# FFN matmuls of 128 x 128 as two column halves of 64, implied waits left out, first loads in parts

## The chip, the cores and the metric

One core of one Trainium2 chip runs the whole program. The metric is the device time of that program in microseconds (us). A profiled execution gives, beside its time, a trace of every engine: TensorE (PE for its matmuls, PEld for the loads of their stationary operand), VectorE (DVE), ScalarE (ACT), GpSimd (POOL) and SyncE (SP), which issues most of the DMAs.

## The reference

Attention with a threshold for 8 sequences of 8 heads (576 tokens, 64 wide), and an FFN with an ELU over all 4608 tokens.

```python
scores = scale * np.matmul(q, k.transpose(0, 1, 3, 2))
thresh = np.max(scores, axis=-1, keepdims=True) - tau
scores = np.where(scores >= thresh, scores, -1000000000.0)
scores = scores - np.max(scores, axis=-1, keepdims=True)
attn = np.exp(scores)
attn = attn / (np.sum(attn, axis=-1, keepdims=True) + 1e-09)
x = np.matmul(attn, v)            # then (B, S, H*D): 4608 x 512
h = x @ w_in                      # 512 x 2048
g = np.where(h > 0.0, h, np.exp(np.minimum(h, 0.0)) - 1.0)
return g @ w_out                  # 2048 x 512
```

## The kernel before

All is fp32. A sequence has four pairs of heads, so there are 32 pairs. Of the 576 tokens, 512 are four blocks of 128 and 64 are the tail; the tails of all eight sequences together make a ninth FFN group (`xtail`).

**Attention.** A step takes 128 queries of a pair. PE writes the scores to PSUM (`scores`, L494, in the first sequence; `wide_scores`, L769, and the tails, L816, later), in tiles of 64 rows by 64 columns: the two heads stand on different rows of the array, and the 128 queries are two halves of 64 columns, so up to four tiles lie side by side. DVE takes the negated maximum (L518, L776), POOL makes the threshold `th` from it (L522, L782), ACT the exponential (L528, L786), DVE masks and sums (L538, L790), POOL or ACT divides. The result is transposed by DVE and a trip through DRAM (`turn_squares`, `fetch`), or by PE (`turn_parts`), and multiplied with the values (`values`, L708 and L713; `tails_and_values`, L821 and L829). L713 and L829 write 64 columns for each head, so two matmuls of 128 rows by 64 columns lie side by side. L708, ahead of L713, covers both heads with a block-diagonal `vd` of 128 by 128.

**FFN.** The first pairs' FFN (`ffn1`, `ffn1_block`, `ffn2_plain`) is plain. From about 256 us on each group of 512 tokens goes through `first_product` (L1447: seven products of 2 x 2 blocks in place of eight, after Strassen and Winograd) and `second_round` (L1587, likewise); for the last groups `deep_product` (L1961, one level deeper, products of 128 columns) and `plain_product` (L2023). Each product is matmuls of 128 x 128 weights by 256 or 128 columns into a PSUM bank, then copies and sums on ACT, DVE and POOL. In the profile one fp32 matmul is two MATMUL records and two LDWEIGHTS.

**Order of the work.** Every engine runs its instructions in the order in which the program lists them. For the first sequence and the pairs up to the ninth the order is the string `EARLY`, one entry a job: `ld.tail.1.0` is the load of the k tails, `ld.k.0.0:act` a load issued by ACT, `idle17@f0` 17 transposes of the identity that only keep PE running, `first.q.0.0@f0` a transpose into bank f0, `sc.n` the scores of step n, `th.n.h` a threshold (its first engine, POOL, unless the entry names one). After that, a schedule by planned times (`at`, `until`, `on_pe`) lays FFN quarters between the attention steps: for each pair, tails and values, the scores of two blocks, FFN, the scores of the other two, FFN.

**Waits.** An instruction that reads or writes the wide PSUM tile is registered by `on_banks` (L720), which makes it wait for the other engines' accesses to the same bank. An instruction with more waits than it can carry gets an EVENT_SEMAPHORE instruction ahead of it on its queue.

**First loads.** `load_one` (L1108) gives source and place of a load; `load_job` (L1123) makes a job of it, on SP or ACT. Before, q of a block and the tails of q or k come in one load for all eight heads.

Of the kernel before, what the change touches and what calls it, by code (L numbers as in the profile page):

```python
# [60 lines left out]
ld.tail.1.0 ld.k.0.0:act ld.k.0.1 ld.tau.0.0:act idle17@f0 ld.q.0.0 ld.k.1.1 ld.k.1.0 lw.0 lw.1 first.t.k.0@f0  # L61
# [115 lines left out]
def kernel(  # L177
# [12 lines left out]
    P = 128  # L190
# [268 lines left out]
    WBUFS = 3  # L459
    e_both, e_next = att.tile([P, 2, 2, HALF], FP32, name="e", bufs=1), [0]  # L460
# [59 lines left out]
    def bound_of(pr, i, h):  # L520
        st = open_steps[pr, i]
        nc.gpsimd.tensor_scalar(st["th"][:, h : h + 1], st["mx"][:, h : h + 1], -1.0, ntau, ALU.mult, ALU.add)  # L522

    def exp_of(pr, i, h):
        st = open_steps[pr, i]
        e = e_slot()
        o = st[h][:, :, :HALF]
        on_banks(nc.scalar.activation(e, o, AF.Exp, bias=st["mx"][:, h : h + 1]), o)  # L528
        st[h] = st[h], e
# [169 lines left out]
    def values(pr, part, pv=None, block=None):  # L699
        b, j = divmod(pr, NPAIR)  # L700
        vm, vd = (raws[pr][x] for x in ("vm", "vd"))
        wT = wTs.pop((pr, part) if block is None else (pr, "block", block))
        if b not in xts:
            xts[b] = xpool.tile([P, KJ, MAIN], FP32, name="xt")
        n = wT.shape[1] * T
        if pv is None:
            pv = granted[0]
        watch(nc.tensor.matmul(pv[:, :n], vd, wT[:, :, NC], start=True, stop=False, skip_group_check=True), pv[:, :n])  # L708
        for c in range(NC):
            for h in range(2):  # L710
                g0, g1 = (2 * h, 2 * h + 10) if part else (0, wT.shape[1])
                o = pv[h * D : (h + 1) * D, g0 * T : g1 * T]
                watch(nc.tensor.matmul(o, vm[:, h, c], wT[:, g0:g1, h * (NC + 1) + c], start=False, stop=(c == NC - 1),  # L713
                                       skip_group_check=True), o)
        return lambda e="act": values_out(pr, part, pv, block, e)

    seen = const.tile([P, 1], FP32, name="seen")
    accesses, banked, doing, after = {}, {}, [None], [()]

    def on_banks(made, ap):  # L720
# [11 lines left out]
        needed += [i for y in after[0] for i in banked.get(y, {}).values() if str(i.engine) != engine and i not in needed]  # L732
        if doing[0]:
            banked.setdefault(doing[0], {})[engine] = ins
# [6 lines left out]
        tc.add_to_no_dep_group(engine, ins)  # L741

# [37 lines left out]
    def wide_bounds(pr, i):  # L780
        st, cs = open_steps[pr, i], slice(0, len(heads_of(i)))
        nc.gpsimd.tensor_scalar(st["th"][:, cs], st["mx"][:, cs], -1.0, ntau, ALU.mult, ALU.add)  # L782
# [277 lines left out]
    def early_tasks():  # L1060
# [47 lines left out]
        def load_one(what, z, h):  # L1108
# [3 lines left out]
            if what == "q":  # L1112
                return w_out_sb[:, NPAIR + z].rearrange("p (h d) -> p h d", d=D), q[0, :, z * P : (z + 1) * P].rearrange("h p d -> p h d")
            if what == "tail":
                return first_tails("qk"[z]), (q, k)[z][0, :, MAIN:].rearrange("h t d -> t h d")
# [19 lines left out]
        for c in range(NC):  # L1135
            load_job("q", c)
        load_job("tail", 0), load_job("tail", 1), load_job("tau")
        job("tau", "dve", lambda e: read_tau(), "ld.tau.0.0")
        for pr in range(NPAIR):
            for name, part, cs in (("k", 0, range(NC)), ("q", 0, (0,)), ("q", 1, (1, 2, 3))):  # L1140
# [3 lines left out]
                    *[("ld", "k", pr, h) for h in range(2) if name == "k"], *[("ld", "q", c, 0) for c in cs if name == "q"],  # L1144
                    bank=("prep", name, pr, part))
                job(("prep", name, pr, part), "act|dve", lambda e, loc=loc: loc["out"](e), x, "tau" if name == "q" else None)
            for z, name in enumerate("qk"):
                loc = {}
                job(("first", "t", name, pr), "pe", lambda e, pr=pr, name=name, loc=loc: loc.update(out=turn_first_tail(name, pr)),
                    ("ld", "tail", z, 0), bank=("copy", name, pr))  # L1150
                job(("copy", name, pr), "act|dve", lambda e, loc=loc: loc["out"](e), ("first", "t", name, pr), "tau" if name == "q" else None)
# [37 lines left out]
        for n in range(per_seq):  # L1189
# [6 lines left out]
            for h in hs:  # L1196
# [4 lines left out]
                job(("th", n, h), "pool", lambda e, pr=pr, i=i, h=h: bound_of(pr, i, h), ("max", n, h), "tau")  # L1201
# [69 lines left out]
        for z, (pr, what) in enumerate((pr, what) for pr in range(NPAIR, START) for what in ("tail", 0, 1)):  # L1271
# [23 lines left out]
            for s, (i, hs, wb) in enumerate(group_steps):  # L1295
# [6 lines left out]
                job(("bth", pr, i), "pool", lambda e, pr=pr, i=i: wide_bounds(pr, i), *[("bmax", pr, i, h) for h in hs])  # L1302
# [80 lines left out]
    with tc.manual_schedule():  # L1383
# [42 lines left out]
        def first_product(g, u):  # L1426
# [6 lines left out]
            def product(k):  # L1433
# [12 lines left out]
                for j in range(2):  # L1446
                    nc.tensor.matmul(loc["banks"][place], left[:, j], right[:, j], start=(begins and j == 0), stop=(j == 1),  # L1447
                                     skip_group_check=True)
# [108 lines left out]
        def second_round(g, r):  # L1557
            banks_ = []

            def chunk(c):  # L1560
# [5 lines left out]
                def quarter(m, k):  # L1566
# [15 lines left out]
                    for v in range(2 * k, 2 * k + 2):  # L1582
# [4 lines left out]
                        nc.tensor.matmul(place(m), lhs, rhs, start=(begins and v == 0), stop=(v == RU - 1),  # L1587
                                         skip_group_check=True)
# [352 lines left out]
        def deep_product(q):  # L1941
# [9 lines left out]
            def p(k):  # L1951
# [8 lines left out]
                for v in range(2):  # L1960
                    nc.tensor.matmul(loc["x"][place][:, :P], left[:, v], right[:, v], start=(begins and v == 0), stop=(v == 1),  # L1961
                                     skip_group_check=True)
# [49 lines left out]
        def plain_product(q):  # L2012
# [3 lines left out]
            def p(c, k):  # L2016
# [5 lines left out]
                for v in range(2 * k, 2 * k + 2):  # L2022
                    nc.tensor.matmul(loc[c][:, :HM], lefts(g, r, c, m)[:, v], rights(r, m)[:, v], start=(v == 0), stop=(v == RU - 1),  # L2023
                                     skip_group_check=True)
# [107 lines left out]
```

## Time and profile before

| | us |
|---|---|
| median of 3 runs | 1264.27 |
| lowest, highest | 1262.33, 1265.05 |
| the profiled execution | 1262.88 |
| its span, first to last instruction | 1261.1 |
| granted clock of TensorE | 1.000 |

In the profile, a line such as "L1447 PE MATMUL f<-xt,sw 128*128 128x256 f32 x512" names the line of the kernel, the engine, the operation, the tiles written and read, the rows and columns of the array in use, the result's partitions and columns, and the number of records. The chain of waits is followed back from the last instruction: at each step to what released it, or to the instruction before it on its engine. Matmuls are pipelined and their ends are modelled; their starts are not, so intervals between starts are the safer measure.

### The profile page before, as it was taken

To read this page: it belongs to the slowest core of one execution; us is meant where nothing else is said; L and a number is where in the kernel's file an instruction comes from. 1 tells how busy PE (TensorE), PEld (TensorE's weight loads), DVE (VectorE), ACT (ScalarE), POOL (GpSimd) and SP (SyncE) were. 2 spreads that over 40 slices of the span, in tenths; PEclk is the share of its full clock that TensorE was granted. 3 is DMA by queue.
4 is the path that set the end of the run, shared out by engine and by line. 5 is a ranking of instruction groups with operands and counts; after the bars stand their busy time and mean duration, and the time that the engine had idled before them with its cause. 6 is when DMAs were issued, how large, how long until landed. Compare 5 with 4: busy or idle time off the path is not lost.

```text
span 1261.1 us, 24668 instructions
## 1 busy us (share of the span) xinstructions
PE 1245.4 (99%) x8187; PEld 970.9 (77%) x8187; DVE 1068.6 (85%) x2322; ACT 584.7 (46%) x1276; POOL 788.6 (63%) x1147
## 2 busy tenths in 40 slices
PE   8999999999999999999999999999999999999998
PEld 5776576477777777777788777777777778899998
DVE  6998989898889979898989888988989885777876
ACT  7987755453444435252625353444535260434130
POOL 5775545586576747674767657674757473675554
PEclk9999999999999999999999999999999999999999
DMA  9568898898989898999889898989889876434433
GB/s 225 147 180 240 226 260 244 240 306 213 254 212 262 233 244 223 260 245 237 241 225 268 218 268 202 269 221 251 215 255 248 237 215 219 166 133 150 143 107 112
DMA packets 332880, 277.84 MB, mean 220 GB/s; under 512 B 201296, under 2 KB 288336, under 8 KB 332752
## 3 DMA queue, kind: packets, MB, share of 16 engines
q1 hardware_dynamic: 331760, 275.73, 78.8%
q8 instruction: 65, 1.06, 0.3%
q10 hardware_dynamic: 992, 0.53, 0.1%
q14 instruction: 63, 0.52, 0.1%
HBM read 178.85 MB, written 97.32 MB: 219 GB/s over the span
## 4 chain that ended last, share of the span: by engine, by line
PE 82%; DVE 3%; issue 1%; ACT 0%; DMA 0%; SPq 0%; POOL 0%; DVEq 0%; ACTq 0%
PE f L1447 30%; PE f L1587 23%; PE sc L829 9%; PE sc L769 8%; PE f L1961 4%; PE f L2023 3%; PE sc L821 1%; PE f L888 1%; PE sc L816 1%; DVE mx L776 1%; PE f L956 1%; DVE x L641 1%; DVE e L790 0%; DVE w_one L790 0%; DMA there<-x 0%
## 5 line engine op out<-in xcount | busy, mean ns | idle before, releaser
L776 DVE TENSOR_REDUCE mx<-sc 128x1 f32<-128x576 f32 x252 | 180.2, 746 | 37.8 <-PE sc L769 32.3
L782 POOL TENSOR_SCALAR th<-mx,ntau 128x2 f32<-128x2 f32 (+1 forms) x140 | 46.0, 329 | 187.1 <-DVE mx L776 186.9
L786 ACT ACTIVATE w_one<-sc,mx 128x576 f32<-128x576 f32 x140 | 100.8, 741 | 132.7 <-DVE mx L776 113.3
L790 DVE SCALAR_TENSOR_TENSOR w_one<-sc,th,w_one 128x576 f32<-128x576 f32 x140 | 110.0, 813 | 20.4 <-ACT w_one L786 20.2
L769 PE MATMUL sc<-kT,qT 64*64 64x256 f32 (+5 forms) x1792 | 124.2, 410 | 2.4 <-DVE su L546 0.5
L1447 PE MATMUL f<-xt,sw 128*128 128x256 f32 x512 | 123.8, 384 | 0.6 <-ACT xt L432 0.5
L786 ACT ACTIVATE e<-sc,mx 128x576 f32<-128x576 f32 x112 | 82.8, 743 | 86.6 <-DVE mx L776 85.0
L1447 PE MATMUL f<-x,w_in_sb 128*128 128x256 f32 x512 | 122.8, 382 | 0.0
L1447 PE MATMUL f<-xt,w_in_sb 128*128 128x256 f32 x512 | 121.2, 379 | 0.5 <-DVE xt L1056 0.5
L769 PEld LDWEIGHTS sc<-kT,qT 64*64 64x64 f32 x1792 | 80.7, 132 | 48.3 <-issue 18.2
L502 POOL TENSOR_SCALAR w_one<-w_one,rs 128x576 f32<-128x576 f32 x115 | 89.4, 788 | 38.7 <-DVE rs L552 38.7
L641 DVE STREAM_TRANSPOSE x<-w_one 128x512 f32<-128x512 f32 (+1 forms) x140 | 99.9, 744 | 14.2 <-POOL w_one L502 9.5
L1447 PEld LDWEIGHTS f<-xt,sw 128*128 128x128 f32 x512 | 94.1, 190 | 21.1 <-issue 5.8
L1447 PEld LDWEIGHTS f<-x,w_in_sb 128*128 128x128 f32 x512 | 96.2, 190 | 16.2 <-ACT g L1508 3.6
L1447 PEld LDWEIGHTS f<-xt,w_in_sb 128*128 128x128 f32 x512 | 97.2, 190 | 14.0 <-ACT e L786 0.8
L790 DVE SCALAR_TENSOR_TENSOR e<-sc,th,e 128x576 f32<-128x576 f32 x112 | 87.7, 808 | 8.3 <-ACT e L786 7.9
L1587 PE MATMUL f<-w_out_sb,g 128*128 128x256 f32 x384 | 92.0, 382 | 0.0
L1587 PE MATMUL f<-w_out_sb,s 128*128 128x256 f32 x384 | 91.9, 382 | 0.0
L1587 PE MATMUL f<-t,s 128*128 128x256 f32 x384 | 90.7, 379 | 0.0
L1587 PEld LDWEIGHTS f<-w_out_sb,g 128*128 128x128 f32 x384 | 72.0, 190 | 13.1 <-issue 3.8
L1587 PEld LDWEIGHTS f<-w_out_sb,s 128*128 128x128 f32 x384 | 71.9, 190 | 12.7 <-issue 3.2
L502 POOL TENSOR_SCALAR e<-e,rs 128x576 f32<-128x576 f32 x92 | 67.8, 742 | 20.8 <-DVE rs L552 18.3
(344 smaller groups left out, 2894.1 us busy)
## 6 DMA issues: line engine op xcount, KB each, us to landing
there<-x SPq DMA_DIRECT2D x452, 144.0 KB, 3.8
wTb<-there SPq DMA_DIRECT2D x58, 576.0 KB, 6.4
wTa<-there SPq DMA_DIRECT2D x55, 576.0 KB, 4.7
sw<-win_sums SPq DMA_DIRECT2D x62, 384.0 KB, 4.3
t<-wout_sums SPq DMA_DIRECT2D x45, 512.0 KB, 5.3
there<-x SPq DMA_DIRECT2D x112, 80.0 KB, 1.9
wTb<-there SPq DMA_DIRECT2D x56, 160.0 KB, 3.6
wst<-in_moe_w_in_dram SPq DMA_DIRECT2D x16, 512.0 KB, 4.8
```

The costliest lines, as they stand in the source:

```text
L502: nc.gpsimd.tensor_scalar(wv, wv, st["rs"][:, h : h + 1], 1.0, ALU.mult, ALU.mult)
L641: nc.vector.transpose(x[:, :, c0 : c0 + nc_], src.rearrange("p (c g n) -> p g c n", c=nc_, n=T))
L769: on_banks(nc.tensor.matmul(oy, qT[r, i * P + y * D : i * P + (y + 1) * D], kT[r, k0 : k0 + n], start=True, stop=True, skip_group_check=Tr ...
L776: on_banks(nc.vector.tensor_reduce(st["mx"][:, h : h + 1], st["sc", h], axis=AX.XY if i == NC else AX.X, op=ALU.max, negate=True), st["sc" ...
L782: nc.gpsimd.tensor_scalar(st["th"][:, cs], st["mx"][:, cs], -1.0, ntau, ALU.mult, ALU.add)
L786: on_banks(nc.scalar.activation(st["e", h], st["sc", h], AF.Exp, bias=st["mx"][:, h : h + 1]), st["sc", h])
L790: on_banks(nc.vector.scalar_tensor_tensor(st["e", h], st["sc", h], st["th"][:, h : h + 1], st["e", h], ALU.is_ge, ALU.mult, accum_out=st[" ...
L829: on_banks(nc.tensor.matmul(o, vm[:, h, c], parts[part][:, g0:g1, h * (NC + 1) + c], start=False, stop=(c == NC - 1), skip_group_check=Tru ...
L1447: nc.tensor.matmul(loc["banks"][place], left[:, j], right[:, j], start=(begins and j == 0), stop=(j == 1), skip_group_check=True)
L1587: nc.tensor.matmul(place(m), lhs, rhs, start=(begins and v == 0), stop=(v == RU - 1), skip_group_check=True)
L1961: nc.tensor.matmul(loc["x"][place][:, :P], left[:, v], right[:, v], start=(begins and v == 0), stop=(v == 1), skip_group_check=True)
L2023: nc.tensor.matmul(loc[c][:, :HM], lefts(g, r, c, m)[:, v], rights(r, m)[:, v], start=(v == 0), stop=(v == RU - 1), skip_group_check=True)
```

## The change

It has four parts.

1. FFN matmuls go through the new `by_columns`, which makes two matmuls of 128 rows by 64 columns of one of 128 by 128. This holds for `first_product` (L1447), `second_round` (L1587), `deep_product` (L1961), `plain_product` (L2023), and for the first matmul of `values` (L708). The moving operand is read by both halves.
2. `on_banks` drops a wait that another one implies, by the new `followed`; and in `exp_of` the dependence on the exponential that used the same slot before is dropped, since a mask lies between.
3. The loads of q's first block and of the k tails are split: heads 0 and 1, then heads 2 to 7. The first line of `EARLY` is rearranged for it.
4. Thresholds may be made by ACT (`bound_of`, `wide_bounds`); no entry of `EARLY` asks for it.

```diff
 EARLY = """
-ld.tail.1.0 ld.k.0.0:act ld.k.0.1 ld.tau.0.0:act idle17@f0 ld.q.0.0 ld.k.1.1 ld.k.1.0 lw.0 lw.1 first.t.k.0@f0
+ld.tail.1.1 ld.k.0.0:act ld.k.0.1 ld.q.0.1:act ld.tau.0.0 ld.tail.1.2:act idle17@f0 ld.q.0.2 ld.k.1.1 ld.k.1.0 lw.0 lw.1 first.t.k.0@f0
...
     def exp_of(pr, i, h):
         st = open_steps[pr, i]
         e = e_slot()
         o = st[h][:, :, :HALF]
-        on_banks(nc.scalar.activation(e, o, AF.Exp, bias=st["mx"][:, h : h + 1]), o)
+        made = nc.scalar.activation(e, o, AF.Exp, bias=st["mx"][:, h : h + 1])
+        if slot_exps[e_next[0]]:
+            tc.declare_no_dep(made.ins, slot_exps[e_next[0]].name, reason="its mask lies between")
+        slot_exps[e_next[0]] = made.ins
+        on_banks(made, o)
...
-        watch(nc.tensor.matmul(pv[:, :n], vd, wT[:, :, NC], start=True, stop=False, skip_group_check=True), pv[:, :n])
+        by_columns(pv[:, :n], vd, wT[:, :, NC], watch, start=True, stop=False)
...
+    serials, known = {}, {}
+
+    def followed(ins, engine, needed):
+        have = known.setdefault(engine, {})
+        kept_ = []
+        for x in needed:
+            e, n, _ = serials[x.name]
+            if n > have.get(e, -1) and not any(serials[y.name][2].get(e, -1) >= n for y in needed if y is not x and serials[y.name][0] != e):
+                kept_.append(x)
+        for x in kept_:
+            e, n, seen = serials[x.name]
+            for z, m in {**seen, e: n}.items():
+                have[z] = max(have.get(z, -1), m)
+        serials[ins.name] = engine, len(serials), dict(have)
+        return kept_
...
+        needed = followed(ins, engine, needed)
...
+    def by_columns(o, left, right, note=None, **how):
+        n = o.shape[0]
+        for y in range(0, n, D):
+            oy = o[y : y + D] if n > D else o
+            made = nc.tensor.matmul(oy, left[:, y : y + D] if n > D else left, right, skip_group_check=True, **how)
+            if note:
+                note(made, oy)
...
             if what == "q":
-                return w_out_sb[:, NPAIR + z].rearrange("p (h d) -> p h d", d=D), q[0, :, z * P : (z + 1) * P].rearrange("h p d -> p h d")
+                hs = (slice(0, H), slice(0, 2), slice(2, H))[h]
+                return w_out_sb[:, NPAIR + z].rearrange("p (h d) -> p h d", d=D)[:, hs], q[0, hs, z * P : (z + 1) * P].rearrange("h p d -> p h d")
...
                 for j in range(2):
-                    nc.tensor.matmul(loc["banks"][place], left[:, j], right[:, j], start=(begins and j == 0), stop=(j == 1),
-                                     skip_group_check=True)
+                    by_columns(loc["banks"][place], left[:, j], right[:, j], start=(begins and j == 0), stop=(j == 1))
```

The replacements at L1587, L1961 and L2023 are of the same form.

41 lines of the change are left out of this document (24 added, 17 removed).

## The prediction

> **What bounds the kernel now.** I read the busy line and the chain of waits on the page first, then the busy time by stages, then the chain in order of time, and last single stretches of the timeline of TensorE.
>
> ```profile
> PE 1245.4 (99%) x8187; PEld 970.9 (77%) x8187; DVE 1068.6 (85%) x2322; ACT 584.7 (46%) x1276; POOL 788.6 (63%) x1147
> PE 82%; DVE 3%; issue 1%; ACT 0%; DMA 0%; SPq 0%; POOL 0%; DVEq 0%; ACTq 0%
> 300.00:700.00 400.00, 400.00 (x2651) 314.23 (x2652) 351.32 (x774) 175.08 (x384) 261.29 (x395) 1.00 0.90 241
> 700.00:1038.00 338.00, 338.00 (x2206) 266.45 (x2200) 294.31 (x647) 147.91 (x323) 216.61 (x329) 1.00 0.86 236
> ```
>
> The columns of the two stage rows are the stretch, its length, and the busy time of PE, PEld, DVE, ACT and POOL. From 300 to 1038 us PE is busy in every microsecond, DVE in 351.32 of 400 (88%). The granted clock is 1.00. The chain names PE with 82%. So from 300 us on the time is the sum of what TensorE streams and of what it loses between streams, and a change to TensorE's work counts one for one. The chain in order of time (start, length, what) gives the period:
>
> ```profile
> 219.76 1.53 DVE w_one L790 x4
> ...
> 320.21 4.03 PE sc L829 x32
> 324.24 2.09 PE sc L769 x24
> 326.33 12.30 PE f L1447 x56
> 338.63 2.09 PE sc L769 x24
> ...
> 1117.28 1.73 PE f L2023 x8
> 1119.01 1.34 PE f L1961 x12
> ```
>
> One pair of heads is values, scores, FFN, scores, FFN. An fp32 matmul leaves two records. A 256-column record takes 1.73/8 = 0.216 us in L2023, a 128-column one 1.34/12 = 0.1117 us in L1961. Each of these runs begins with a change of the array's shape, and what such a beginning costs is seen in the timeline of PE. A matmul's end is modelled, so I take the start-to-start interval: the length of a row less one matmul (0.38 us at 256 columns), over the intervals in it.
>
> ```profile
> 964.83 0.38 PE L1447 MATMUL f<-x,w_in_sb 128*128 128x256 f32 x1
> 965.14 0.45 PE L816 MATMUL sc<-kT,qT 64*64 64x288 f32 x1
> ...
> 965.96 0.38 PE L821 MATMUL sc<-wTa,vd 64*64 64x256 f32 x1
> 966.27 2.38 PE L829 MATMUL sc<-wTb,vm 128*64 128x320 f32 x16
> 968.47 1.90 PE L829 MATMUL sc<-wTa,vm 128*64 128x256 f32 x16
> 970.30 2.49 PE L769 MATMUL sc<-kT,qT 64*64 64x448 f32 x32
> ...
> 972.72 1.56 PE L1587 MATMUL f<-w_out_sb,g 128*128 128x256 f32 x6
> ...
> 974.55 1.46 PE L1587 MATMUL f<-t,g 128*128 128x256 f32 x6
> ```
>
> Three things are in these rows. First, a change of shape costs 0.09 us whichever way it goes: 964.83 to 965.14 and 965.96 to 966.27 are each 0.31 where a 256-column record has 0.216. Second, the first 128*128 run loses more behind it: (1.56 - 0.38)/5 intervals sum to 1.18 against 5 x 0.216 = 1.08, so 0.10 us is lost once, while the later row has (1.46 - 0.38)/5 = 0.216 and loses nothing. That is the first weight load, which has nothing to hide behind. Third, column halves are already in this kernel: L829 works on 128*64, two halves side by side. Its 16 records of 256 columns are 8 pairs, (1.90 - 0.38)/7 = 0.217 us for a pair, the same as one 128*128 record. Its first row, after a change of shape, has 7 intervals in 2.38 - 0.44 = 1.94; at 0.217 x 320/256 = 0.271 they would take 1.89, so only 0.05 us is lost there.
>
> **The change part by part.**
>
> (a) FFN runs in column halves. In the steady stretch a pair of halves takes what one record took (0.217 against 0.216), so 0. At the beginning of a run the exposed load falls from 0.10 to 0.05: the means of one load say the same.
>
> ```profile
> L1447 PEld LDWEIGHTS f<-xt,sw 128*128 128x128 f32 x512 | 94.1, 190 | 21.1 <-issue 5.8 <-DMA there<-x 1.2 <-ACT xt L432 0.9
> L829 PEld LDWEIGHTS sc<-wTa,vm 128*64 128x64 f32 x448 | 32.2, 137 | 19.2
> ```
>
> That is 190 against 137 ns, 0.053 less. The chain has 44 such runs of 56 between the two rows here (two every 34.0 us, 22 pairs):
>
> ```profile
> 292.38 12.31 PE f L1587 x56
> ...
> 1021.09 12.44 PE f L1447 x56
> ```
>
> 44 x 0.053 = 2.3 us. The change of shape itself stays: scores work on 64*64 and FFN on 128*64 after it, and 64*64 to 128*64 at 966.27 costs the same 0.09.
>
> (b) Eleven runs take 12.44 instead of 12.30. The extra 0.14 sits inside them, where a wait on ACT lets the queue of loads run dry:
>
> ```profile
> 957.13 2.03 PE L1447 MATMUL f<-x,w_in_sb 128*128 128x256 f32 x8
> ```
>
> 7 intervals in 2.03 - 0.38 = 1.65 against 1.51. About 0.10 of the 0.14 is again an exposed load, and half of it goes: 11 x 0.053 = 0.6 us, if ACT is no later than now (0 if it is).
>
> (c) Where values are followed directly by FFN, 128*64 meets 128*64 and the change of shape goes too. From 1037.64 + 1.03 - 0.38 = 1038.29 to 1038.61 are 0.32, so 0.10, and the load behind it, 0.10: 0.2 us once.
>
> ```profile
> 1037.64 1.03 PE L829 MATMUL sc<-wTa,vm 128*64 128x256 f32 x8
> 1038.61 1.56 PE L1587 MATMUL f<-w_out_sb,g 128*128 128x256 f32 x6
> ```
>
> (d) The 128-column products of L1961 take 0.1117 us a record. Pairs of halves of that size are in the first sequence:
>
> ```profile
> 27.15 0.49 PE L708 MATMUL sc<-wTa,vf 128*128 128x128 f32 x2
> 27.57 1.09 PE L713 MATMUL sc<-wTa,vm 128*64 128x128 f32 x16
> 1100.00:1253.00 153.00, 56.62 (x476) 56.38 (x476) 1.00 0.40 129
> ```
>
> (1.09 - 0.28 - 0.05)/7 = 0.109 us a pair, 0.0027 less, and the last row counts 476 records of L1961: 1.2 us. At the ends: 0 and 2 us.
>
> (e) The first matmul of the early values (L708, 24 records) becomes halves, so the change of shape between it and L713 and its own exposed load go: its two records take 0.42 (27.15 to 27.57) where two pairs at a beginning need 0.22 + 0.05, and L713 behind them has no beginning of its own any more (0.05): 0.20 us x 12 = 2.4 us of PE. Before 280 us the chain also runs over DVE (219.76 above), so between 0 and 2.4 lies on the path; I take 0.4, the low side, because filler transposes of the identity stand in that stretch and take up what comes free.
>
> (f) First loads in parts. The head 0/1 parts of q and of the k tails land earlier, but PE has no use for them earlier:
>
> ```profile
> 1.46 3.89 PE L555 MATMUL f<-ident 128*128 128x128 f32 x17 [1.46 <-POOL ident masks.py:199]
> 4.38 0.15 DVE L240 TENSOR_SCALAR pos<-tau_sb 128x1 f32<-128x1 f32 x1 [4.38 <-DMA tau_sb<-in_tau_dram]
> 5.27 0.18 PEld L405 LDWEIGHTS f<-ident,w_out_sb 64*128 64x128 f32 x1 [0.33 <-issue]
> 6.24 0.60 PE L555 MATMUL f<-ident 128*128 128x128 f32 x4
> 6.67 0.73 PE L555 MATMUL f<-ident,w_out_sb 128*128 128x128 f32 x2
> 6.98 0.37 ACT L426 ACTIVATE x<-f,keep 128x128 f32<-128x128 f32 x1
> 7.54 0.71 PE L494 MATMUL sc<-x 64*64 64x288 f32 x8
> ```
>
> The 17 fillers last until 5.35 by the model and hold the first real transpose at 5.27 whatever has landed; the 4 fillers hold q's at 6.67, and both fillers stay. So 0 for the loads. What is moved: ACT issues two more loads (0.5 us each, before its first copy), SP takes tau's after two others, about 1 us later, so L240 starts near 5.4 and its five operations end near 6.2, still ahead of 6.98, where ACT first needs them. SP has one load more in all, so weight loads behind it issue about 0.5 us later. Cover gone, that is at worst 0.7 us; if q was late after all, up to 0.5 us gain. I take 0.
>
> (g) Implied waits left out: an instruction with two waits has an extra one on its queue ahead of it.
>
> ```profile
> L769 PEldq EVENT_SEMAPHORE  x18: 51/51/51, 131.1 to 970.5; - x18
> L816 PEldq EVENT_SEMAPHORE  x16: 51/51/51, 143.0 to 963.1; - x16
> L790 DVEq EVENT_SEMAPHORE  x88: 21/21/21, 120.6 to 1010.6; - x88
> ```
>
> At most 34 x 0.051 = 1.7 us on PE and 88 x 0.021 = 1.8 us on DVE. On PE the one before 965.14 hides in the 0.31 of the change of shape; DVE has its 12% of idle time from 300 us on. I take 0.3, of 0 to 1.7. The choice of engine for the bounds is not used: no entry of the order names it.
>
> **Sum:** 2.3 + 0.6 + 0.2 + 1.2 + 0.4 + 0 + 0.3 = 5.0 us. The profiled execution took 1262.88 us (span 1261.1 and 1.8 around it), so 1257.9; it lies 1.4 under the median of 1264.27, from which the sum is 1259.3. I forecast 1259.
>
> **The rivals.**
>
> *TensorE's queue cannot issue that fast (slower).* Loads and matmuls double: 4 instructions a pair. At 256 columns that is 54 ns each, at 128 columns in L1961 27 ns each. The fastest stretch of the trace:
>
> ```profile
> 290.20:291.90 1.70, 1.70 (x30) 1.37 (x32) 1.34 (x5) 0.53 (x2) 1.70 (x2) 1.00 0.80 218
> ```
>
> 30 matmuls and 32 loads in 1.70 us are 27 ns an instruction, for 62 of them. Over a whole run of scores (32 matmuls, as at 970.30, and as many loads, in the 2.09 us of the chain) it is 32.7 ns. If that were the limit, a pair in L1961 would cost 4 x 32.7 = 131 ns, 19 more than now, x 476 = 9.1 us, against the 3.8 us of (a), (b), (c), (e) and (g): 1264.3 + 5.3 = 1269.6. It decides from 4 x 30 = 120 ns on, where 476 x 0.008 eats the rest. For it: no run of 27 ns longer than 62 instructions is in the trace. Against it: the scores are bound by what they stream, not by issue, so 32.7 is only the slowest that the limit can be.
>
> A rule of the Trainium skill speaks for this rival (TensorE: Matmul & The Clock Gate, Part 2): the sequencer may spend about 62 ns on each MATMUL, which binds when the array's work on one is shorter. Two halves would then cost 124 ns, 12 more than L1961 now, an estimated 5.9 us on 476, and the sum would be 1266.4. The trace speaks against it for short runs: L713's eight pairs took 109 ns each.
>
> *The gain is turned into waits (no change).* From 300 to 1038 us DVE works 88% of the time and waits for ACT already sit in eleven runs (b). If each period is held by such a wait, what PE saves there becomes idle time of PE, and only what lies behind 1038 us stays: (c) and (d), 1.4 us, 1264.3 - 1.4 = 1262.9. For it: (b). Against it: PE has no idle time in 738 us, and the saving is 0.12 us in a period of 34.
>
> *More of the early part counts.* If PE is the bound before 280 us after all, (e) gives 2.4, (g) 1.7 and (f) 0.5: 3.9 us more than in the sum, 1255.4. For it: PE stands in the chain there too. Against: so does DVE, and the fillers keep PE busy with nothing.
>
> *The halves do not overlap in FFN.* L829 has its two halves on different moving data; in FFN both stream the same. If they ran one after the other, 3136 records of 256 columns (L1447 and L1587) would cost 0.216 us more each, over 600 us. Only L829 and L713 speak on it, and both overlap; 1 in 100.
>
> **How the numbers follow.** Forecast 0.62, more of the early part 0.10, turned into waits 0.17, queue 0.10, no overlap 0.01. The forecast's own range is 1256.5 to 1261.5, from (b), (d), (e) and (g) at their ends and the 1.4 us between profile and median. The range for 8 in 10 takes in the early case below and the case without change above, and leaves out the queue: 1254.5 to 1265. About 0.2% (2.5 us) is what a measurement of this kernel can tell from no change; below 1261.7 is faster. Forecast and early case lie there, but for the upper edge of the forecast: 0.72. The case of waits is the same, with the edges: 0.17. Slower: 0.11, the queue and the case without overlap.
>
> **What would show it.** (a): in the chain, L1587 and L1447 runs of 12.25 instead of 12.30, the same 0.217 a pair within, mean load near 137 ns, and 0.31 still between scores and FFN. (b): the eleven long runs at 12.39 or below. (c): no gap at 1038. (d): L1961 at 0.109 a pair; 0.12 or more is the queue. (e): 128*128 gone from L708 and no 0.09 between it and L713. (f): the first score still at about 7.5 us. (g): fewer waits of 51 ns in L769 and L816. Wrong would be: idle time of PE between 300 and 1038 us, or an interval within FFN over 0.22 us.

## The result, and the profile after

The changed kernel takes 1259.09 us (median of 6 runs, 1258.30 to 1259.56) where the kernel before, in 6 runs beside it, takes 1263.76: a ratio of 0.9965, with a 95% interval from 0.9955 to 0.9974. (The ratios here and below, to which the intervals belong, are not the quotients of the medians; that would be 0.9963 here.) The forecast was 1259.0. The profiled execution took 1258.30 us with a span of 1256.5, which is 4.6 less than the span of before. Both profiled executions are among the shorter ones of their kernel.

The busy line and the chain's shares come from the page of the changed kernel, the last two rows from its busy time by stages.

```profile
PE 1240.8 (99%) x11999; PEld 825.9 (66%) x11999; DVE 1067.2 (85%) x2322; ACT 584.4 (47%) x1276; POOL 790.5 (63%) x1147
PE 81%; DVE 2%; DMA 1%; POOL 1%; ACT 0%; issue 0%; SPq 0%; DVEq 0%; ACTq 0%; POOLq 0%
...
300.00:700.00 400.00, 399.89 (x3970) 253.79 (x3968) 351.42 (x775) 175.27 (x385) 262.54 (x396) 1.00 0.89 242
700.00:1034.00 334.00, 334.00 (x3294) 212.52 (x3292) 291.88 (x644) 147.16 (x320) 213.81 (x324) 1.00 0.87 237
```

TensorE issues 3812 matmuls more and is still, nearly everywhere, what the time is the sum of. Weight loads take 145 us less of busy time, but they were hidden before: only the first load of a run was not. Every matmul that goes through `by_columns` stands at one line now, L772; L802 are the scores, L852 and L857 the tails, L865 the values, L563 the transposes. The chain in order of time (start, length, what) shows a period and the end of the steady part:

```profile
319.08 4.03 PE sc L865 x32
323.11 2.09 PE sc L802 x24
325.20 12.25 PE f L772 x112
337.45 2.09 PE sc L802 x24
339.54 12.35 PE f L772 x112
...
1031.70 4.03 PE sc L865 x32
1035.73 24.17 PE f L772 x224
```

Values and scores are what they were (4.03 and 2.09). An ordinary FFN run went from 12.30 to 12.25, a long one from 12.44 to 12.35. The timeline of TensorE (start, length, engine, line, what, count) shows where the 0.05 is:

```profile
963.18 0.38 PE L857 MATMUL sc<-wTa,vd 64*64 64x256 f32 x1
963.49 2.38 PE L865 MATMUL sc<-wTb,vm 128*64 128x320 f32 x16
965.69 1.90 PE L865 MATMUL sc<-wTa,vm 128*64 128x256 f32 x16
967.52 2.55 PE L802 MATMUL sc<-kT,qT 64*64 64x448 f32 x32
970.00 1.95 PE L772 MATMUL f<-w_out_sb,g 128*64 128x256 f32 x16
971.77 1.90 PE L772 MATMUL f<-t,g 128*64 128x256 f32 x16
...
1033.84 1.90 PE L865 MATMUL sc<-wTa,vm 128*64 128x256 f32 x16
1035.56 1.68 PE L772 MATMUL f<-w_out_sb,g 128*64 128x256 f32 x14
```

The FFN row at 970.00 is the first of a run: 7 intervals in 1.95 - 0.38 = 1.57, where the row behind it has 1.52. So 0.05 is lost at the beginning where it was 0.10, and within the run a pair of halves takes 1.52/7 = 0.217. Single starts say the same for all 45 runs between 290 and 1062 us: from the first product of a run to the second it is 0.320 us in the kernel before and 0.267 here (0.216 at 1035.56, see below), and 0.216 from the second to the third in both. The change of shape stays at 0.31 (963.18 to 963.49, and from 965.69 + 1.90 - 0.38 = 967.21 to 967.52). At 1035.56 there is none: 1033.84 + 1.90 - 0.38 = 1035.36, and 0.20 later FFN begins, an ordinary interval.

At the end of the program stand the products of 128 columns:

```profile
1235.87 0.64 PE L772 MATMUL f<-t,e 128*64 128x128 f32 x8
1236.30 0.64 PE L772 MATMUL f<-x,e 128*64 128x128 f32 x8
1236.74 0.64 PE L772 MATMUL f<-t,wTb 128*64 128x128 f32 x8
1237.17 0.64 PE L772 MATMUL f<-x,wTb 128*64 128x128 f32 x8
1237.61 1.93 PE L772 MATMUL f<-w_out_sb,s 128*64 128x256 f32 x16
```

Four groups of four pairs lie between 1235.87 and 1237.61: 1.74/16 = 0.109 us a pair, where one whole record took 0.1117.

To see where the time was won, I subtract, for the same row of scores or values, its start in the kernel before from its start here. All profiled kernels are in one table; their edits are in the next section. Columns are the times of those rows in the kernel before, in us, and the last one is the span.

| kernel | 7.5 (first score) | 35.6 | 131 | 270 | 286 | 407 | 422 | 1034.6 | span 1261.1 |
|---|---|---|---|---|---|---|---|---|---|
| changed | -0.43 | -0.75 | -1.06 | -1.39 | -1.09 | -1.40 | -1.48 | -2.94 | -4.6 |
| changed, again | -0.33 | -0.64 | -0.91 | -1.39 | -0.02 | -0.32 | -0.29 | -0.85 | -2.5 |
| halves alone | +0.29 | +0.30 | +0.26 | +0.19 | -0.09 | -0.47 | -0.55 | -2.32 | -3.7 |
| waits alone | +0.29 | -0.03 | -0.35 | -0.60 | +0.90 | +1.23 | +1.23 | +1.19 | +0.7 |
| loads alone | +0.44 | +0.44 | +0.46 | +0.50 | +0.06 | +0.04 | +0.04 | -0.00 | -0.4 |
| loads alone, again | +0.15 | +0.16 | +0.13 | +0.14 | -0.06 | -0.08 | -0.08 | -0.05 | -0.6 |
| changed, fillers | -0.67 | +0.16 | -0.15 | -0.63 | -1.15 | -1.50 | -1.58 | -2.98 | -4.6 |
| halves in all FFN | +0.50 | +0.16 | +1.01 | +1.69 | +1.47 | +1.15 | +2.72 | +2.89 | +1.1 |
| all but `ffn1_block` | +0.05 | -0.27 | -0.23 | +1.06 | +1.86 | +1.56 | +1.92 | +0.59 | -1.1 |
| quarters | -0.33 | -0.66 | -0.50 | +0.65 | +0.11 | -0.25 | +3.62 | +3.46 | +5.4 |
| quarters, again | +0.33 | +0.11 | +0.28 | +0.13 | -0.41 | -0.81 | +0.79 | -0.57 | +0.1 |

Two executions of one program can lie far apart in span (2.1 us for the changed kernel, 5.3 for the quarters), so a row tells where time moves, and the medians what it is worth. The execution of before that all rows are compared with took 1262.88 us, about 1 us less than that kernel's medians (1263.76 to 1264.27), so a kernel whose row runs level with it can still be 1 us faster by the median. The first row gives the four shares of the 4.6 us: 1.09 up to 286 us, 1.85 in the steady part up to 1034.6, 0.20 at the meeting of values and FFN near 1036, and the last 1.46 behind it.

The early part has its own two changes. The start, up to the first score, and the values of the first sequence:

```profile
2.79 2.36 PE L563 MATMUL f<-ident 128*128 128x128 f32 x11
...
5.29 0.65 PE L563 MATMUL f<-ident,w_out_sb 128*128 128x128 f32 x4
...
7.11 1.20 PE L495 MATMUL sc<-x 64*64 64x288 f32 x16
...
26.55 0.44 PE L772 MATMUL sc<-wTa,vf 128*64 128x128 f32 x4
26.82 1.04 PE L721 MATMUL sc<-wTa,vm 128*64 128x128 f32 x16
```

The first matmul of the values takes 0.27 (26.55 to 26.82) where it took 0.42, and the sixteen behind it (1.04 - 0.28)/7 = 0.109 a pair, with nothing lost at their beginning. And these are the waits that are issued as instructions of their own, with count and least, median and longest duration in ns; the last row is of the kernel before and has no counterpart here:

```profile
L802 PEldq EVENT_SEMAPHORE  x14: 51/51/51, 173.8 to 967.8; - x14
L852 PEldq EVENT_SEMAPHORE  x15: 51/51/51, 142.3 to 960.3; - x15
L826 DVEq EVENT_SEMAPHORE  x88: 21/21/21, 119.7 to 1007.7; - x88
```

```profile
L528 ACTq EVENT_SEMAPHORE  x32: 17/17/38, 14.3 to 101.7; - x32
```

TensorE lost five of its 34, VectorE none of the 88 ahead of its masks, ScalarE all 32 ahead of the first exponentials. Two more kinds went that no step of the prediction names: VectorE's six ahead of its maxima (L776 before) and 22 of ScalarE's 120 ahead of the later exponentials (L786 before). The halves brought new ones: 189 ahead of VectorE's additions (`add`), where there were 143.

### The profile page after: what moved, and what is told of

It is laid out like the page before. It is cut to its first block, busy times and chain, and to the rows that moved or that the text cites. A ratio compares the mean times of both kernels' runs of the same rounds, so it can differ in the third digit from the quotient of the medians.

```text
span 1256.5 us, 32264 instructions
## 1 busy us (share of the span) xinstructions
PE 1240.8 (99%) x11999; PEld 825.9 (66%) x11999; DVE 1067.2 (85%) x2322; ACT 584.4 (47%) x1276; POOL 790.5 (63%) x1147
## 4 chain that ended last, share of the span: by engine, by line
PE 81%; DVE 2%; DMA 1%; POOL 1%; ACT 0%; issue 0%; SPq 0%; DVEq 0%; ACTq 0%; POOLq 0%
PE f L772 59%; PE sc L865 9%; PE sc L802 8%; PE f L992 2%; PE sc L857 1%; DMA there<-x 1%; PE sc L852 1%; PE f L924 1%; DVE mx L809 1%; DVE e L826 0%; DVE x L649 0%; DVE g L1536 0%; DVE g L1508 0%; SPq L668 0%; SPq L683 0%
## 5 line engine op out<-in xcount | busy, mean ns | idle before, releaser
L802 PE MATMUL sc<-kT,qT 64*64 64x320 f32 (+5 forms) x1792 | 124.5, 410 | 2.1 <-DVE su L554 0.5
L772 PE MATMUL f<-xt,sw 128*64 128x256 f32 x1024 | 123.3, 382 | 0.7 <-ACT xt L432 0.5
L772 PE MATMUL f<-x,w_in_sb 128*64 128x256 f32 x1024 | 123.1, 380 | 0.3 <-ACT g L1547 0.3
L772 PE MATMUL f<-xt,w_in_sb 128*64 128x256 f32 x1024 | 121.8, 379 | 0.5 <-DVE xt L1092 0.5
L802 PEld LDWEIGHTS sc<-kT,qT 64*64 64x64 f32 x1792 | 80.9, 132 | 48.9 <-issue 18.5
L772 PE MATMUL f<-w_out_sb,s 128*64 128x256 f32 (+1 forms) x896 | 105.6, 377 | 0.0
L772 PE MATMUL f<-w_out_sb,g 128*64 128x256 f32 (+1 forms) x864 | 101.7, 376 | 0.0
L772 PEld LDWEIGHTS f<-x,w_in_sb 128*64 128x64 f32 x1024 | 74.4, 137 | 37.9 <-ACT g L1547 4.8
L772 PEld LDWEIGHTS f<-xt,w_in_sb 128*64 128x64 f32 x1024 | 75.4, 137 | 35.9 <-ACT e L822 0.9
L772 PEld LDWEIGHTS f<-xt,sw 128*64 128x64 f32 x1024 | 71.9, 137 | 41.1 <-issue 5.5
L772 PE MATMUL f<-t,s 128*64 128x256 f32 (+1 forms) x800 | 93.5, 375 | 0.0
L772 PEld LDWEIGHTS f<-w_out_sb,s 128*64 128x64 f32 x896 | 63.7, 137 | 31.5 <-issue 3.2
L772 PEld LDWEIGHTS f<-w_out_sb,g 128*64 128x64 f32 x864 | 61.2, 137 | 31.7 <-issue 3.7
```

The lines of the kernel that those rows point to most:

```text
L772: made = nc.tensor.matmul(oy, left[:, y : y + D] if n > D else left, right, skip_group_check=True, **how)
L802: on_banks(nc.tensor.matmul(oy, qT[r, i * P + y * D : i * P + (y + 1) * D], kT[r, k0 : k0 + n], start=True, stop=True, skip_group_check=Tr ...
```

## The experiments

**Each part alone.** Three kernels, each the kernel before with one part of the change.

Column halves (part 1 of the change, and nothing else):

```diff
-        watch(nc.tensor.matmul(pv[:, :n], vd, wT[:, :, NC], start=True, stop=False, skip_group_check=True), pv[:, :n])
+        by_columns(pv[:, :n], vd, wT[:, :, NC], watch, start=True, stop=False)
...
-                    nc.tensor.matmul(loc["banks"][place], left[:, j], right[:, j], start=(begins and j == 0), stop=(j == 1),
-                                     skip_group_check=True)
+                    by_columns(loc["banks"][place], left[:, j], right[:, j], start=(begins and j == 0), stop=(j == 1))
```

Expected:

> The kernel before with the column halves alone (FFN and the first matmul of the values); waits and loads as before. If the halves carry the gain by exposed weight loads and the 128-column products: 44 runs of FFN at 12.25 us instead of 12.30, the long ones at 12.35, the 128-column pairs at 0.109, the part behind 1034 us shorter by 1.5 us, in all 3.5 us less than before (ratio 0.9972), and the first score still at 7.54 us. If the waits and loads carry it: ratio 0.999 or above.

Measured: 1259.51 us beside 1263.93, ratio 0.9974 (0.9964 to 0.9984). The quotient of the medians is 0.9965. In the table its difference is nearly the same at the first score and at 131 us (+0.29 and +0.26), so the shorter values of the first sequence are worth 0.03 and not 2.4; from 286 to 1034.6 us it falls by 2.23, near 1036 by 0.20, behind that by another 1.2. The first score came at 7.83 us, not at 7.54; see (f) below. What follows: the halves carry most of the gain, 4.4 of 4.7 us by the medians and about three quarters by the ratios (0.26% of 0.35%).

Waits (`followed`, and the dependence between exponentials of one slot):

```diff
+        needed = followed(ins, engine, needed)
...
+        if slot_exps[e_next[0]]:
+            tc.declare_no_dep(made.ins, slot_exps[e_next[0]].name, reason="its mask lies between")
```

Expected:

> The kernel before with the implied waits left out alone. If these waits are on the path of the first sequence: each score step of the first 60 us comes some 0.05 us earlier than the one before it did, 0.4 us by 60 us and 0.8 us by 255 us, and 0.5 to 0.8 us in the time (ratio 0.9995). If they are hidden, the start times agree within 0.1 us and the ratio is 1.000. First score at 7.54 us in both.

Measured: 1263.38 beside 1263.93, ratio 0.9997 (0.9988 to 1.0005). The trace says more than the ratio: from +0.29 the difference falls by 0.06 at each of the first score steps and reaches -0.60 at 270 us, a gain of 0.89; at 286 us it is +0.90. So in this execution the gain is there at 270 us and does not reach the end.

Loads (the split loads and the first line of `EARLY`), twice:

```diff
-ld.tail.1.0 ld.k.0.0:act ld.k.0.1 ld.tau.0.0:act idle17@f0 ld.q.0.0 ld.k.1.1 ...
+ld.tail.1.1 ld.k.0.0:act ld.k.0.1 ld.q.0.1:act ld.tau.0.0 ld.tail.1.2:act idle17@f0 ld.q.0.2 ld.k.1.1 ...
```

Expected, the first time and the second:

> The kernel before with the first loads in parts alone. If the loads bring the first score forward: it starts at about 7.1 us, 0.4 us earlier, and the time is 0.4 us less. If instead the fillers hold it and what differed was when TensorE reached its full rate (matmuls of the fillers at 0.21 us against 0.11 us): the first score is at 7.54 us or wherever the step of the rate puts it, with loads that landed earlier all the same.

> The kernel before with the first loads in parts alone, once more. If the loads gain what the first time showed: ratio 0.999 again, with an interval below 1. If that was how its executions happened to fall: 0.9995 to 1.0005. The first score lies between 7.1 and 8.1 us in both, wherever TensorE's step to its full rate falls.

Measured: 1262.49 beside 1263.93, ratio 0.9988 (0.9980 to 0.9997), then 1262.66 beside 1263.79, ratio 0.9995 (0.9986 to 1.0003). Both traces run level with the kernel before from 286 us on. The two intervals overlap and the second reaches 1, so no gain of the loads is established. None is ruled out either: both medians are lower than that of the kernel before, by 1.44 and 1.13 us, about what the execution compared with in the table is short of its own median, and by the ratios up to 0.12% of the 0.35% may come from here. The first score stood at 7.98 and 7.68 us, later than in the kernel before (7.54).

**The changed kernel again**, to know the spread:

> The changed kernel once more, to be compared with e7_not_blocks on the same chip: 1259 us, ratio 0.9965. Its first score at another place than 7.11 us if that hangs on the step of TensorE's rate and not on the loads; the starts behind 286 us follow the landing of the DMA at 265 us.

Measured: 1259.05 beside 1263.79, ratio 0.9966 (0.9954 to 0.9979). The median holds to 0.04 us, while its profiled execution is 2.1 us longer than the other one. The table says where: it too is at -1.39 at 270 us, but at -0.02 at 286.

**What happens between 255 and 286 us.** In the chain of the changed kernel this stretch does not lie on TensorE:

```profile
253.61 1.79 PE sc L802 x18
255.42 0.77 DVE mx L809 x2
...
264.40 4.37 DMA there<-x
...
275.85 1.47 DVE e L826 x4
...
278.64 5.40 PE f L772 x48
```

The scores hand over to DVE and POOL, these to a store into the scratch in DRAM that needs 4.37 us to land, and TensorE gets its next work at 278.64. In the kernel with the waits alone the same store took longer:

```profile
264.96 5.72 DMA there<-x
```

In the second execution of the changed kernel it landed in 4.46 us, but SyncE issued it only at 265.38, behind other DMAs. The landing is 1.07 us later there than in the first execution, and so are the starts at 286 us (-0.02 against -1.09), as the expectation had it.

So there are two ways through the stretch, one over TensorE and one over DVE and DRAM, and the later one decides. To test it I made TensorE later on purpose, with more fillers in the changed kernel near 20 us:

```diff
-su.1:act sc.2 end.0 norm.0.1:act shift.2 prep.k.3.0 rec.1 part.0.1@f2 norm.1.1 max.2.0 sign.1 idle21@f1 max.2.1
+su.1:act sc.2 end.0 norm.0.1:act shift.2 prep.k.3.0 rec.1 part.0.1@f2 norm.1.1 max.2.0 sign.1 idle35@f1 max.2.1
```

> The changed kernel with 14 more filler transposes of the identity in the first sequence, near 34 us (35 in place of 21); nothing else differs. At 0.109 us each they put 1.5 us on TensorE, which is in the chain there. Theory (the stretch from 255 to 287 us is held by DVE and by a trip through DRAM, and swallows what the first 250 us gain or lose, up to 1 us or so): the starts are 1.5 us later than in the changed kernel up to 250 us, so near those of the kernel before, and from 287 us on the difference is at most 0.5 us beside its two profiles; the median is 1259.1 to 1259.7. Rival (the early 1 us of waits left out counts at the end as well): still 1.5 us later at 287 us, and a median of 1260.6.

Measured: 1260.05 (9 runs, 1258.25 to 1261.90) beside 1264.27, ratio 0.9971 (0.9961 to 0.9981). The fillers stand near 20 us and not near 34, and made the starts 0.95 us later, not 1.5: from -0.58 at 17 us to +0.37 at 21. At 270 us this kernel is 0.76 behind the changed one, at 286 us it is level with it (-1.15 against -1.09), and its profiled span is the same 1256.5. Its chain through the stretch lies on TensorE, behind 261 us without a break:

```profile
259.87 0.58 DVE xt L1092
...
260.59 8.95 PE f L772 x80
269.54 2.09 PE sc L802 x24
271.62 12.36 PE f L772 x112
```

What follows: in the trace, a loss of 0.76 us ahead of 255 us was swallowed whole. The times don't show it: the median lies between the two expectations, the interval holds both, and the ratio is 0.0005 to 0.0006 above the two of the changed kernel, some 0.7 us of the 0.95 that the fillers put in. So for the mean over executions it stays open how much the stretch swallows. In the traces, what the first 250 us gain does not reach the end in full: of 1.39 us here 1.09 were left behind the stretch, in the second execution 0.02.

**Halves in the early FFN too.** The change left three places alone: `ffn1`, `ffn1_block` and `ffn2_plain`. First all three in halves, then all but `ffn1_block`:

```diff
-                nc.tensor.matmul(cur[c, i][:, :DM], hidden(c, ft % NU, 1)[:, 0, ft // NU, i], w_out_sb[:, ft],
-                                 start=(ft == 0), stop=(ft == NFT - 1))
+                by_columns(cur[c, i][:, :DM], hidden(c, ft % NU, 1)[:, 0, ft // NU, i], w_out_sb[:, ft],
+                           start=(ft == 0), stop=(ft == NFT - 1))
```

> The changed kernel with the halves in the first pairs' FFN too (ffn1, ffn1_block, ffn2_plain). If exposed loads are the cost there as well: 17 beginnings at 0.053 us and 256 records of 128 columns at 0.0025 us, 1.5 us of TensorE before 256 us, of which about half is on the path: 0.7 us less than the changed kernel (ratio to before 0.996). If DVE is the bound there: as the changed kernel (0.9965).

> The changed kernel with the halves in ffn1 and ffn2_plain too, but not in ffn1_block, whose neighbours are transposes on the whole array. If what cost e4_all_ffn its 2 us was the change of shape beside these transposes: starts up to 158 us differ from the changed kernel by the first score alone, and from 158 to 255 us 9 beginnings at 0.05 us and one change of shape are saved: 0.4 us earlier, and the time 0.4 us less than the changed kernel or the same. If halves cost something by themselves there: as e4_all_ffn, 2 us more.

Measured: 1261.13 beside 1263.93, ratio 0.9982 (0.9973 to 0.9991), and 1261.53 beside 1263.79, ratio 0.9979 (0.9970 to 0.9988). Each is some 2 us worse than the changed kernel, and leaving out `ffn1_block` did not help. The largest loss that both have stands between 131 and 158.6 us (158.6 is no column of the table: the first kernel goes from +1.01 to +2.56 there, the second from -0.23 to +1.33), where `ffn2_plain` alternates with transposes. First the changed kernel, then that with halves:

```profile
134.41 0.60 PE L563 MATMUL f<-ident,e 128*128 128x128 f32 x4
134.84 1.88 PE L992 MATMUL f<-w_out_sb,g 128*128 128x512 f32 x4
136.56 0.60 PE L563 MATMUL f<-ident,e 128*128 128x128 f32 x4
```

```profile
135.29 0.66 PE L563 MATMUL f<-ident,e 128*128 128x128 f32 x4
135.87 1.94 PE L772 MATMUL f<-w_out_sb,g 128*64 128x512 f32 x8
137.74 0.66 PE L563 MATMUL f<-ident,e 128*128 128x128 f32 x4
```

From one group of transposes to the next it is 2.15 us in the one and 2.45 in the other: 0.30 for two changes of shape and two exposed loads. (By single starts, the first product behind the change of shape comes 0.09 us late on the way into FFN, from 135.67 to 135.87, and 0.10 late on the way out, from 137.21 to 137.74; each time the next interval is another 0.05 too long.) Transposes work on 128*128, so an FFN on 128*64 beside them adds a change of shape on each side, where beside the scores of 64*64 the change was there anyway. Six such groups between 131 and 158 us make 1.8 us, against 1.56 found. The first of the two kernels lost 1.6 us more between 407 and 422 us and as much near 555 us, each time to a wait for weight sums from DRAM; those are not in the second, so they are no part of this.

**Quarters of 32 columns**, to look for the limit of issue, twice (the second for a second profile):

```diff
-        for y in range(0, n, D):
-            oy = o[y : y + D] if n > D else o
-            made = nc.tensor.matmul(oy, left[:, y : y + D] if n > D else left, right, skip_group_check=True, **how)
+        for y in range(0, n, T):
+            oy = o[y : y + T]
+            made = nc.tensor.matmul(oy, left[:, y : y + T], right, skip_group_check=True, **how)
```

> The changed kernel with its FFN matmuls in four parts of 32 columns instead of two of 64. Instructions double again: 8 for a 128-column product, 13.6 ns each in 0.109 us. If TensorE's queue is not the limit and only the exposed load counts: 0.216 us for a group of four at 256 columns, 0.11 at 128 columns, a beginning at 0.05 us or less, time within 1.5 us of the changed kernel (1259). If the issue of instructions is the limit at 30 ns each: 0.24 us a group, 11% more, and over 60 us more in all.

> The kernel with quarters (matmuls of 128 rows by 32 columns) once more, for a second profile. Theory (quarters stream as fast as halves, and the 6.8 us that it lost are stalls, above all a late load of weight sums with a lower clock behind it): the intervals of products are again 0.216 us at 256 columns and 0.109 at 128, and the stalls over 0.3 us stand at other places or have other lengths than at 417, 1136, 1144 and 1185 us. Rival (a limit of quarters themselves, in issue or in fetching instructions): stalls of the same length at the same places.

Measured: 1265.89 (10 runs, 1262.41 to 1269.28) beside 1263.79, ratio 1.0018 (1.0007 to 1.0028); the second time one execution of 1263.10. The products stream at the same rate as halves, here those of 128 columns at the end of the program:

```profile
1244.00 0.65 PE L772 MATMUL f<-x,wTb 128*32 128x128 f32 x16
1244.43 0.65 PE L772 MATMUL f<-w_out_sb,wTb 128*32 128x128 f32 x16
1244.87 1.13 PE L772 MATMUL f<-x,kT 128*32 128x128 f32 x31
```

Four products in 0.435 us: 0.109 each, with four matmuls and four loads in it, so on average a matmul every 27 ns and an instruction every 14. Most of the loss is stalls. One is a wait for weight sums from DRAM, and behind it the granted clock fell to about a half (the timeline's row, then busy time by stages, whose next to last three columns are the clock, the DMA share and GB/s):

```profile
416.83 2.53 PE L772 MATMUL f<-xt,sw 128*32 128x256 f32 x32 [2.06 <-DMA sw<-win_sums]
```

```profile
416.80:418.00 1.20, 1.17 (x24) 0.74 (x28) 0.35 (x2) 0.00 (x0) 0.61 (x1) 1.00 1.07 371
418.00:421.20 3.20, 3.20 (x36) 1.59 (x32) 2.16 (x5) 1.36 (x4) 1.19 (x2) 0.51 1.09 310
421.50:424.00 2.50, 2.50 (x52) 1.49 (x48) 1.44 (x2) 1.24 (x3) 1.45 (x3) 1.00 0.56 97
```

From 407 to 422 us this kernel lost 3.87 us: some 2.2 of waiting (2.06 by the row) and 1.6 of half speed. The second execution waited there too, 1.48 us, and its clock stayed at 1.00. The others are stalls that nothing in the trace releases, the page's "issue", three of them with 2.1 us in all in the first execution between 1130 and 1190 us, two with 1.2 in the second (3.9 and 2.1 of the 10.0 us between the profiled spans of the first and of the changed kernel; the other 4 are spread and were not taken apart):

```profile
1184.77 0.31 PE L772 MATMUL f<-x,wTb 128*32 128x128 f32 x4 [0.63 <-issue]
```

Each of the five ends 1.2 to 1.5 us after a packet on the queue that brings instructions had landed. Here are that queue's rows (packets, MB, share), of the changed kernel and of the quarters:

```profile
q8 instruction: 94, 1.54, 0.5%
```

```profile
q8 instruction: 154, 2.52, 0.9%
```

TensorE running out of instructions would fit this, but most of the packets have no such stall behind them, and no run tries it alone. Of the expectation for the second profile, the rate held and the stalls did not move as foretold: the wait near 416 us and a stall at the same point of the program near 1180 came again. So streaming does not limit quarters; whether the fetching of their own instructions does stays open.

## Why the prediction was right, step by step

**(a) Exposed loads, 2.3 us.** Right, and the size nearly so. An ordinary run lost 0.05 as foretold (12.30 to 12.25); in the table a pair of runs gains 0.04 to 0.05 each. Quarters bear the reason out: at the beginnings of the runs, the first interval is 0.320 us in the kernel before, 0.267 with halves and 0.240 with quarters, where a stream has 0.216. So 0.104, 0.051 and 0.024 us are exposed: it goes with the width of the load. The rival without overlap is out: within a run a pair of halves takes 0.216 to 0.217 us.

**(b) Runs with an inner wait, 0.6 us.** Right in kind, mis-sized. Beyond what (a) counts for them, the eleven long runs gain 0.035 to 0.04 each (0.085 in all, 12.44 to 12.35), so 0.4 us. The bound named, 12.39 or below, held. The steady part of the halves alone gives 2.23 where (a) and (b) were 2.9: 44 x 0.047 + 11 x 0.038 = 2.5 less 0.3 that came back as short waits, such as 0.08 at the beginning of the runs near 834 and 902 us. In the changed kernel one wait of 0.27 us near 618 us comes on top (for DVE's addition into `g`, L1508, itself late behind a store and POOL), hence 1.85 there. That is the rival "gain turned into waits" with a small share: some 0.3 to 0.6 of 2.5 us.

**(c) Values straight into FFN, 0.2 us.** Right: 0.20, and no gap in the trace at 1035.56.

**(d) Products of 128 columns, 1.2 us.** Right in size (0.0027 x 476 is 1.3; the sum has 1.2). 476 x (0.1116 - 0.1092), the means of the intervals in both traces, are 1.1 us. Why a pair of halves is 2% shorter than one whole product at 128 columns, and not at 256, no run shows. Of the 1.46 us that the end of the program gained, 0.27 is a stall at 1225.6 us in the profiled execution of before; the three kernels without halves, too, gain 0.4 to 0.5 there, so some 1.0 is left for the halves. Queue issue, the rival on the slow side, is out: a pair did not take 131 ns but 109. The Trainium skill's rule (TensorE: Matmul & The Clock Gate, Part 2), some 62 ns where the sequencer decodes each MATMUL, does not bind here; quarters hold 27 ns a matmul on average. The Trainium skill, in the same part of that page, puts a floor of some 25 ns under the distance of two matmuls. The mean of 27 ns lies above it, but single starts do not: the two halves of a product begin 7 ns apart (1065.527 and 1065.534 us), so for tiles side by side the floor does not hold here.

**(e) First matmul of the early values, 0.4 of 0 to 2.4.** The 0.20 us of PE came as worked out (0.15 at L772 and 0.05 behind it), and 0.03 in all reached the starts behind it. The low side was right, and even it too high: where the chain passes through DVE and through fillers, freed time of TensorE is not time.

**(f) First loads, 0.** Right as to the loads, not as to the first score, which was to stay near 7.5 and came at 7.11. What moved it is in the rows from 2.79 on: four transposes at 5.29 take 0.65 here and 0.83 in the kernel before, because TensorE goes from 0.213 us a transposed block to 0.109 at 4.9 us in the one and at 5.9 in the other. The busy time by stages lists the granted clock as 1.00 in both, but the trace's own record of the full clock begins only at 4.82 us in the one and at 5.97 in the other. The first score follows that moment in all twelve profiled executions, from 6.87 us (full clock at 4.35) to 8.04 (at 7.27), and old and new loads lie on one line: 7.83 behind 6.80 with the old ones, 7.87 behind 6.91 with the new. So the loads don't set this: with the new ones the first score came between 6.87 and 8.04 us in nine executions (mean 7.5), with the old ones at 7.54, 7.83 and 7.83. The Trainium skill (TensorE: Matmul & The Clock Gate, Part 1) has half rate until a free-running window of about 3.4 us has been busy, which would make the moment of the step arbitrary in this way. The trace agrees: every recorded stretch at one clock, up to the last step, is a whole multiple of 3.413 us (1252.69 us of full clock in the changed kernel are 367 of them, 1256.11 in the kernel before are 368).

**(g) Waits left out, 0.3 of 0 to 1.7.** Wrong in mechanism. The gain was to come from 51 ns waits of TensorE; five of 34 went. What the step left out were ScalarE's: 32 waits ahead of the early exponentials, 19 of them in the first 60 us. In that stretch the kernel with the waits alone lost no other waits, and it is there that each score step comes 0.06 us earlier. The waits alone gained 0.89 us up to 270 us, more than 0.3, and lost it again by 286 us. By the ratio they are worth 0.03%, some 0.4 us, with an interval that holds 0, so that the sum's 0.3 was near is luck. How much each wait contributes to the 0.06 at a score step was not taken apart.

Taken together, 3.2 us of the 4.6 in the profiled execution lie in (a) to (d), 1.85 + 0.20 + 1.1, where the forecast had 4.3; 1.1 came through the early part, where it had 0.7 (the first score, 0.43 earlier with the step of the clock, is in it), and 0.3 is a stall of the execution compared with. In the second execution of the changed kernel the early part brought 0.02, so the rival by which more of the early part counts has no support. The sum of 5.0 us is somewhat too large: the medians differ by 4.7, and 0.9965 is 4.4. That the median met the forecast to 0.1 us is in part luck: 5.0 was taken from the median of three runs, 1264.27, and from that of all six, 1263.76, it would have given 1258.8; and the profiled spans of the same kernel lie 2.1 us apart.

## What to carry to other kernels

At 256 columns a split matmul streams no faster (at 128 it took 2% less); it pays by the part of the first weight load that nothing hides, and only where its neighbours already work on another shape of the array: beside scores of 64*64 halves won 0.05 us a run, beside transposes of 128*128 they cost 0.30 us a group. Follow a gain through the trace to the next point where the chain leaves the engine; a saving ahead of a wait for DVE and DRAM can be gone there, though each of its instructions got shorter. Differences of start times, row by row against the kernel before, show this where medians cannot.

## What the runs showed of the hardware

- **Column tiles issue faster than the trace of before could show.** A matmul of 128 x 32 every 27 ns on average with a load beside each, over the 128-column products of the end except at stalls and beginnings; the tightest stretch in the trace of before had 62 instructions.
- **A wait of 2.06 us on TensorE was followed by 3.2 us at a granted clock of 0.51**, at 418 us in the first execution of the quarters. By the trace's own record the half clock holds from 418.03 to 421.45 us, 3.41 us. Waits of 1.48 us (quarters, again) and of 1.4 us (halves in all FFN, at 418 and 555 us) were not. The Trainium skill (TensorE: Matmul & The Clock Gate, Part 1) has a window of some 3.4 us for this, which agrees with the length of the slow stretch; it asks for an idle window of that length first, and here only 2.06 of the 3.41 us ahead of the fall were a wait.
- **A change of shape costs 0.09 to 0.11 us in every direction that these traces show.** From the last FFN product of a run to the scores it is 0.309 us in the kernel before, 0.316 with halves and 0.329 with quarters, where a product takes 0.216; from the tails on 64*64 to the values on 128*64 it is 0.31; between 128*64 and the transposes on 128*128 it is 0.09 one way and 0.10 the other. The exposed load comes on top, by its width.
- **The same store lands in different times.** The store into `there` near 264 us took 4.37 us in the changed kernel and 5.72 in that with the waits alone; in the second execution of the changed kernel it took 4.46 and was issued 0.98 us later. In the two executions of the changed kernel the starts at 286 us follow its landing.
